# Turning every block of B.x on ScalarE and DMA: a fused S5 and long-convolution kernel

## The chip, the cores and the metric

One NeuronCore of a Trainium2 chip. The metric is the device time of one execution in microseconds (us), the median of several runs.

## The reference, cut to what matters

With x of 2048 rows and 1024 columns, the result is `g*a + (1-g)*b`:

```
g = sigmoid((x * gate_w).sum(-1))
a = S5(x):   Bu = x @ B_bar^T (complex, 1024 states);  h[t] = Lam_bar*h[t-1] + Bu[t]
             a = 2*Re(h @ C^T) + x*Dskip
b = H3(x):   kv = shift(k)*v;  b = x * (long_conv(kv, ssm_k) + kv*ssm_D)      # FFT of length 4096
```

The recurrence is taken two steps at a time. For a pair of rows the kernel forms `V = even + Lam*odd_before` (complex), scans over the pairs, and rebuilds the other half of the states from the scanned ones. `V` is what this text calls a *turned* block: the even half of `B.x` plus the odd half, one step back, times a complex number per state.

## The kernel before, in words

**Tiles.** x is cut into 4 time blocks (tb) of 512 rows, each split into an even and an odd half of 256 (HB). The states are cut into 4 groups (g) of two tiles (j) of 128. So `B.x` has 16 blocks (tb, g), numbered by `order`: blocks 0 to 5 are (0,0), (0,1), (1,0), (1,1), (2,0), (2,1), then (0,2), (0,3), (1,2), (1,3), (2,2), (2,3), and the last four are time block 3. A block's tile, one j, costs 32 matmuls of 256 columns (as separate halves, names `odd` and `even`) or 16 of 512 columns (name `both`).

**Engines.** TensorE (PE) multiplies; ScalarE (ACT) moves nearly every PSUM result to SBUF; VectorE (DVE) does the products of the spectra and the scans; GpSimd (POOL) issues the DMAs that add to what lies in their destination (`gather`, line 133); SyncE (SP) issues the loads, the transposing loads and the stores. PSUM is one pool of 4 buffers of two banks each (`ps2`), so a PE tile can only start when the buffer four tiles earlier has been copied out.

**Order.** Every instruction is recorded through `put`, which pins it behind the one recorded before it on its engine. So each engine runs in the order in which the program text calls it, written out by hand with generators (`step`, `steps`, `run`): if an instruction waits, all later ones of its engine wait too. All recorded instructions show the one line L94, and are told apart by the names of their tiles.

**First half: the long convolution.** Channel blocks c = 0 to 7 go through `fwd_K` (matmuls `psk`, copied out as `Kh` or `BT`), `fwd_V` (`psv`, copied out as `Vh`), `products(c)` on DVE (the `G`, `wkh`, `t` and `BT` rows), and `inverse(c-1)` (`psz`, copied out as `cv` and stored to the DRAM scratch `cv_scr`). Each turn of the loop has one `mirror` matmul, which waits for DVE's `ks`. Between these lie tiles of `B.x` for blocks 0 to 3 (the generator `parts`) and 4 and 5 (the generator `tiles`).

**How a block is turned.** There are two ways.

- Blocks 0 and 1 (`Bu_tile`): PE itself adds the turned odd half into the PSUM buffer of the even half, by 4 matmuls a tile with diagonal matrices `lamd`. `lam_diag` builds those, 6 of 128x128 for each group: for group 0 on ACT (`on_act`), for group 1 on DVE.
- Blocks 2 to 15: `Bu_halves` or `Bu_plain` copies both halves out plainly as `O_` and `V_`. A later `turn_U` scales the odd half on ACT into two buffers `Q` (2 instructions of 128x512 for the first, 4 of 128x256 for the second), and each Q is added to `V_` by one gather. The second gather of a block waits until the first has landed, since both add to the same bytes. Rows show these as `Q<-U,lam` and `U<-Q`.

**From the last channel block on.** After the loop, block 6 is made by the tiles b6 and b7, block 7 by b8 and b9, block 8 by b10 and b11; blocks 9 to 13 follow as B9 to B13 of `plan`, while the scans begin. Block 8 uses a buffer of the pool `wu` (3 buffers, shared with Q): its first instruction, `U<-ends`, can only run when an earlier buffer's gathers have landed. Then `psy` matmuls multiply the states by C.

**C's tiles.** `turn_C(pi)` turns tile pi of C (128 states) by `mc2i`, `c2r` and `mc2r`: ACT writes two scaled copies m or Q (128x1024 each), then the tile itself is scaled twice, by ACT for pi 0 and 1 and by DVE (`ts`) for the rest; for pi 0, 1, 4, 5 (`by_sum`) the copies are added by two gathers, for the others by DVE. `on_act` is a list of steps of `turn_C` that `Bu_next` takes between tiles of `B.x`.

**Loads.** `load_BT(g, c)` transposes one part (real or imaginary) of a group of B, 256 states, into `BT[g]`.

Of the kernel before, what the change touches and what calls it, by code (L numbers as in the profile page):

```python
# [20 lines left out]
def kernel(  # L21
# [35 lines left out]
    ND = D // 128  # L57
# [187 lines left out]
    def load_BT(g, c, held=False):  # L245
        if held:
            hold(BT[g][:, c, 0, 0:1])
        load_t(BT[g][:, c], (A_B_re, A_B_im)[c][g * 256:(g + 1) * 256, :])

    def load_xT(tb, halves=(0, 1), held=False):  # L250
        if tb not in xTs:
# [515 lines left out]
    order += [(NTB - 1, g) for g in range(NG)]  # L767
    ends = consts.tile([128, 2, NG, 2, 2], BF16, name="ends")

    def lam_diag(g, home, on_act=False):  # L770

        if g == 0:
            lamd["all"] = home.tile([128, 2, 2, 3, 128], BF16, name="lamd", tag="lamd")
        t = lamd[g] = lamd["all"][:, g]
        for j in range(2):
            for k, f in enumerate((lam[:, 0], lam[:, 1], mlam)):
                pi = 2 * g + j
                if on_act:
                    act(t[:, j, k], ident, func=ACT.Identity, scale=f[:, pi:pi + 1])
                else:  # L780
                    ts(t[:, j, k], ident, f[:, pi:pi + 1], None, ALU.mult)

    def Bu(i):
        tb, g = order[i]
        if i == 13:
            V_ = s5p["v13"].tile([128, 2, 2, HB], BF16, name="V13")
            O_ = lam_pool.tile([128, 2, 2, HB + 2], BF16, name="O13", tag="lamd")
            Us[tb, g] = V_, O_[:, :, :, 2:]
            turns_U[i] = turn_U(g, V_, O_)
            return [Bu_plain(tb, g, V_, O_, j) for j in range(2)]  # L790
        if i in (10, 11):
            if i == 10:
                s5p["u2"] = xt_pool.tile([128, 2, 2 * (4 * HB + 4)], BF16, name="U2", tag="xT")
            U = s5p["u2"][:, i - 10]
        else:
            shape = [128, 2 * (4 * HB + 4)]
            if i in (6, 7, 8, 15):
                U = u4(shape, BF16, "U")
            else:
                home = uu[0 if i in (0, 1, 14) else 1] if i < 6 or i == 14 else s5p["uu"]  # L800
                U = home.tile(shape, BF16, name="U")
        if i >= 2:
            V_, O_ = U[:, 0:4 * HB], U[:, 4 * HB:]
            V_ = V_.rearrange("p (c j t) -> p c j t", c=2, j=2)
            O_ = O_.rearrange("p (c j t) -> p c j t", c=2, j=2)
            Us[tb, g] = V_, O_[:, :, :, 2:]
            turns_U[i] = turn_U(g, V_, O_)
            return [(Bu_halves if i < 4 else Bu_plain)(tb, g, V_, O_, j) for j in range(2)]
        U = U[:, 0:8 * HB].rearrange("p (a c j t) -> p a c j t", a=2, c=2, j=2)
        Us[tb, g] = U[:, 0], U[:, 1]  # L810
        return [Bu_tile(tb, g, U, j) for j in range(2)]

    def Bu_tile(tb, g, U, j):
        xT = xTs[tb]
        ps = []
        d = lamd[g][:, j]
        for a in (1, 0):
            ps.append(ps2([128, 2, HB], ("even", "odd")[a]))
            for c in range(2):
                for dt_ in range(ND):  # L820
                    mm(ps[1 - a][:, c], BT[g][:, c, dt_, j * 128:(j + 1) * 128], xT[:, dt_, a * HB:(a + 1) * HB],
                       dt_ == 0 and (a == 1 or c == 0), a == 1 and dt_ == ND - 1)
            if a == 1:
                act(U[:, 1, :, j], ps[0], func=ACT.Copy)
                if j == 1 and tb < NTB - 1:
                    act(ends[:, tb % 2, g], U[:, 1, :, :, HB - 1], func=ACT.Copy)
                yield
        yield
        for k, c, o in ((0, 0, 0), (0, 1, 1), (1, 0, 1), (2, 1, 0)):
            if tb > 0:  # L830
                mm(ps[1][:, o, 0:1], d[:, k], ends[:, 1 - tb % 2, g, c, j:j + 1], False, False)
            mm(ps[1][:, o, 1:HB], d[:, k], U[:, 1, c, j, 0:HB - 1], False, k == 2)
        act(U[:, 0, :, j], ps[1], func=ACT.Copy)
        yield

    turns_U = {}

    def Bu_halves(tb, g, V_, O_, j):
        if j == 0:
            act(O_[:, :, :, 1], ends[:, 1 - tb % 2, g], func=ACT.Copy)  # L840
        for a in (1, 0):
            ps = ps2([128, 2, HB], ("even", "odd")[a])
            for c in range(2):
                for dt_ in range(ND):
                    mm(ps[:, c], BT[g][:, c, dt_, j * 128:(j + 1) * 128], xTs[tb][:, dt_, a * HB:(a + 1) * HB],
                       dt_ == 0, dt_ == ND - 1)
            if a == 1:
                act(O_[:, :, j, 2:], ps, func=ACT.Copy)
                if j == 1:
                    act(ends[:, tb % 2, g], O_[:, :, :, HB + 1], func=ACT.Copy)  # L850
            else:
                act(V_[:, :, j], ps, func=ACT.Copy)
            yield
        yield

    def Bu_plain(tb, g, V_, O_, j):
        xT = xTs[tb]
        if j == 0 and tb > 0:
            act(O_[:, :, :, 1], ends[:, 1 - tb % 2, g], func=ACT.Copy)
        elif j == 0:  # L860
            act(O_[:, :, :, 1], lam[:, :, 0:2], func=ACT.Copy, scale=0.0)
        ps = ps2([128, 2, 2, HB], "both")
        for c in range(2):
            for dt_ in range(ND):
                mm(flat(ps[:, c]), BT[g][:, c, dt_, j * 128:(j + 1) * 128], xT[:, dt_], dt_ == 0, dt_ == ND - 1)
        act(O_[:, :, j, 2:], ps[:, :, 1], func=ACT.Copy)
        if j == 1 and tb < NTB - 1:
            act(ends[:, tb % 2, g], O_[:, :, :, HB + 1], func=ACT.Copy)
        act(V_[:, :, j], ps[:, :, 0], func=ACT.Copy)
        yield  # L870

    def turn_U(g, V_, O_):
        both = slice(0, 2)
        for part in (((both, both, lam[:, 0]),), ((0, 1, lam[:, 1]), (1, 0, mlam))):
            if s5p["Q"] is s5p["wu"]:
                if part[0][0] == both:
                    whole_Q = u4([128, 2, 2, 2, HB], BF16, "Q")
                Q = whole_Q[:, part[0][0] != both]
            else:
                Q = s5p["Q"].tile([128, 2, 2, HB], BF16, name="Q")  # L880
            for j in range(2):
                pi = 2 * g + j
                for c, o, f in part:
                    act(Q[:, o, j], O_[:, c, j, 1:1 + HB], func=ACT.Identity, scale=f[:, pi:pi + 1])
            gather(V_, Q)
            yield
# [211 lines left out]
    step(sp)  # L1098
    run(first)
    dg1 = dgs(1, True)  # L1100
    run(angles)
    load("kT", 1)
    load("v", 1)
    load("kn", 1)
    fwd_K(0, (0, 1))
    fwd_V(0, (0, 1))
    step(sp)
    step(turns)
    taps(1, dg1)
    step(sp)  # L1110
# [21 lines left out]
    for c in range(NC - 1):  # L1132
        n, nn = c + 1, c + 2
        if c == 0:
# [28 lines left out]
            step(apart)  # L1163
            load_xT(0, (1,))
            run(apart)
            lam_diag(0, lam_pool, True)
            continue
        if c == 6:
            put("pool", nc.gpsimd.tensor_copy, stamp, xTs[2][:, 0, 0:HB + 1:HB])
# [1 line left out]
        step(old)  # L1171
        step(tabs)
        if c == 6:
            step(parts)
        step(back)
        step(tv)
        steps(prod, 3)
# [11 lines left out]
        if c == 2:  # L1189
            step(parts)  # L1190
        fwd_K(n, (0, 1))
        if c in (2, 6):
            step(parts)
        fwd_K(n, (2, 3))
        if c == 4:
            step(parts)
# [6 lines left out]
        if nn < NC:  # L1203
# [2 lines left out]
            step(fk)  # L1206
            if c < 5:
                step(fk)
            if c == 4:
                step(parts)  # L1210
            if c == 1:
                load_BT(1, 0, True)
            elif c < 5:
                load("v", nn, True)
            step(parts)
            taps(nn, dg)
            if c == 5:
                load("v", nn)
# [20 lines left out]
        else:  # L1239
            run(next(tiles))  # L1240
            for pi in range(3):
# [2 lines left out]
                    hold(CT[0][:, 0, 0:1])  # L1244
                load_CT(pi)
                if pi == 0:
                    load_BT(2, 0)
                    load_BT(2, 1)
            run(next(tiles))
            run(next(tiles))  # L1250
        fwd_V(n, (0, 1))
        if c < 6 and c != 4:
            step(parts)
            if c in (1, 3):
                step(parts)
        fwd_V(n, (2, 3))
        if c in (4, 5):
            step(parts)
        if c == 1:
            lam_diag(1, lam_pool)  # L1260
        old = tabs

    h3r.close()
# [10 lines left out]
    def turn_C(pi):  # L1274
# [7 lines left out]
            act(m[c], CT[pi][:, 1 - c], func=ACT.Identity, scale=mc2i[:, pi:pi + 1])  # L1282
            yield
        for c, f in enumerate((c2r, mc2r)):
            if pi < 2:
                act(CT[pi][:, c], CT[pi][:, c], func=ACT.Identity, scale=f[:, pi:pi + 1])
            else:
                ts(CT[pi][:, c], CT[pi][:, c], f[:, pi:pi + 1], None, ALU.mult)
            if by_sum:
                gather(CT[pi][:, c], m[c])  # L1290
        if not by_sum:
            tt(CT[pi], CT[pi], whole_m, ALU.add)

    turning = [turn_C(pi) for pi in range(NP)]
    load_BT(3, 0)
    load_BT(3, 1)
    load_CT(3)
    with tc.tile_pool(name="fin", bufs=1, side="right") as fin:

# [5 lines left out]
        prod, back = products(c, 0, room, False), inverse(c - 1)  # L1305
        run(old)
        steps(prod, 3)
        run(turns_U[3])
        run(next(tiles))
        steps(turning[0], 2)  # L1310
        step(back)
        steps(turning[1], 2)
        run(back)
        gate(1)
        gate(2)
        steps(prod, 2)
        b6, b7 = Bu(6)
        run(b6)
        run(b7)
        run(turns_U[6])  # L1320
        run(turning[0])
# [111 lines left out]
    for j in range(NS):  # L1433
# [6 lines left out]
        advance(j)  # L1440
        for t in turning[2 * j:2 * j + 2]:
            run(t)
        on_act += [lambda t=t: step(t) for t in turning[2 * j + 2:2 * j + 4] for _ in range(2)]
        turn = turns_U[turned[j]] if j in turned else none
        if j != 10 and plan[j][0:1] != "G":
            step(turn)
# [82 lines left out]
```

## Time and profile before

| | |
|---|---|
| median of 3 runs | 384.49 us (384.44 to 384.77) |
| the profiled execution | 384.57 us: its span 382.8 us, and 1.8 us around it |
| granted TensorE clock | 0.998 |
| busy PE / DVE / ACT / POOL | 371.3 / 371.2 / 303.6 / 81.8 us |
| DMA | 71.77 MB, 187 GB/s on average |

How to read it: busy time is the sum of the instructions' durations on an engine, and the span is the time from the first instruction to the last. Instructions of one engine overlap at their ends (an ACT row of 0.60 us is followed by the next one 0.49 us after its start), so costs in the text are taken from start to start where a row of the same kind follows. The chain is found by going back from the last instruction to what released it. "Idle before" is time in which an engine did nothing ahead of an instruction, with what ended it.

### The profile page before, as it was taken

Reading aid. Unit: us, or ns where it says so; the run is one execution under the profiler, and the core shown is the slowest. Engines: PE = TensorE matmul, PEld = TensorE weight load, DVE = VectorE, ACT = ScalarE, POOL = GpSimd, SP = SyncE. Lnnn points to the kernel's source line nnn. Section 1 sums busy time; section 2 is a strip of 40 time slices with the busy share of each in tenths; the row PEclk is TensorE's granted clock in tenths of the full one; section 3 lists DMA queues with packets and bytes.
Section 4 is the critical chain, followed back from the end, with each engine's and each line's share of the span. In section 5 each row is a group of like instructions: output and inputs, shape, how many; then the busy total and the mean of one; then the engine's idle time right before and its main releaser. Section 6 shows DMA issues by size and latency. Waiting matters only on the chain.

```text
span 382.8 us, 6633 instructions
## 1 busy us (share of the span) xinstructions
PE 371.3 (97%) x2419; PEld 198.3 (52%) x2453; DVE 371.2 (97%) x599; ACT 303.6 (79%) x469; POOL 81.8 (21%) x108
## 2 busy tenths in 40 slices
PE   7899999999999999999999999989999999999995
PEld 5566458575584846744454444434444444444442
DVE  7999999999999999999999999999999999999996
ACT  5898998988979999786979699675989759937601
POOL 4011030020301102031003110413414323634100
PEclk9999999999999999999999999999999999999999
DMA  7979999998999997959999999986899999898903
GB/s 166 165 108 223 218 205 205 245 203 211 201 164 211 208 213 169 198 125 154 192 221 164 226 203 250 213 153 125 150 222 192 208 245 246 136 250 156 238 8 110
DMA packets 126402, 71.77 MB, mean 187 GB/s; under 512 B 104665, under 2 KB 107489, under 8 KB 126370
## 3 DMA queue, kind: packets, MB, share of 16 engines
q1 hardware_dynamic: 111232, 45.64, 55.4%
q0 software_dynamic: 12976, 25.17, 38.9%
q10 hardware_dynamic: 2162, 0.54, 0.8%
q8 instruction: 19, 0.31, 0.3%
q14 instruction: 13, 0.11, 0.1%
HBM read 15.48 MB, written 8.39 MB: 62 GB/s over the span
## 4 chain that ended last, share of the span: by engine, by line
PE 52%; DVE 30%; issue 9%; DMA 4%; ACT 3%; ACTq 1%; POOL 0%; DVEq 0%; POOLq 0%
PE psy L94 29%; PE both L94 15%; DVE BT L94 11%; DVE wkh L94 8%; DVE G L94 5%; DVE t L94 3%; PE psz L94 2%; DVE ks L94 2%; PE psk L94 2%; DMA CT<-Q 2%; DMA pbb<-cv_scr 1%; PE psv L94 1%; DMA rows<-in_gate_w_dram 1%; PE p L94 1%; PE taps L94 1%
## 5 line engine op out<-in xcount | busy, mean ns | idle before, releaser
L94 PEld LDWEIGHTS <-BT 128*128 128x128 bf16 x640 | 62.0, 98 | 48.3 <-issue 0.2
L94 PE MATMUL both<-xT,BT 128*128 128x512 bf16 x375 | 83.0, 379 | 0.4
L94 POOL DMA_DIRECT2D U<-Q x26 | 26.7, 1039 | 88.8 <-ACT Q L94 31.0
L94 PEld LDWEIGHTS <-hb 128*128 128x128 bf16 x256 | 24.9, 98 | 31.4 <-issue 1.6
L94 PEld LDWEIGHTS <-U 128*128 128x128 bf16 x240 | 23.5, 98 | 28.3
L94 PE MATMUL psy<-CT,hb 128*128 128x512 bf16 x157 | 36.3, 379 | 0.1
L94 ACT ACTIVATE Vh<-psv 128x1024 bf16<-128x1024 f32 x32 | 30.7, 1034 | 5.3 <-PE psv L94 5.3
L94 PE MATMUL psy<-CT,U 128*128 128x512 bf16 x149 | 34.6, 379 | 0.2
L94 ACT ACTIVATE Q<-U,lam 128x512 bf16<-128x512 bf16 (+1 forms) x52 | 29.9, 612 | 4.9 <-DMA CT<-Q 4.9
L94 DVE TENSOR_TENSOR_SCAN W<-rv,init,A 128x256 bf16<-128x256 f32 x48 | 32.2, 730 | 0.0
L94 POOL DMA_DIRECT2D G<-wkh x8 | 9.7, 1218 | 102.8 <-DVE wkh L94 102.8
L94 ACT ACTIVATE U<-both 128x512 bf16<-128x512 f32 x44 | 24.1, 595 | 8.0 <-PE both L94 7.5
L94 PEld LDWEIGHTS <-SF 128*128 128x128 bf16 x184 | 18.0, 98 | 19.7 <-issue 1.4
L94 PE MATMUL psk<-eok,SF 128*128 128x512 bf16 (+1 forms) x119 | 27.9, 354 | 0.3
L94 PE MATMUL psz<-G,CI 128*128 128x512 bf16 x64 | 24.3, 379 | 0.1
L94 PE MATMUL psz<-G,SI 128*128 128x512 bf16 x64 | 24.3, 379 | 0.0
L94 PE MATMUL psy<-CTa,hb 128*128 128x512 bf16 x94 | 22.6, 379 | 1.2 <-ACT U L94 1.0
L94 PE MATMUL taps<-dg,kT 128*128 128x128 bf16 (+1 forms) x352 | 21.7, 210 | 0.8 <-DMA kT<-in_B_k_dram 0.8
L94 PEld LDWEIGHTS <-kT 128*128 128x128 bf16 x352 | 21.0, 100 | 2.5 <-DMA kT<-in_B_k_dram 2.1
L94 DVE TENSOR_TENSOR wkh<-BT,Vh 128x3072 bf16<-128x3072 bf16 (+4 forms) x20 | 21.8, 1110 | 0.0
L94 DVE TENSOR_TENSOR wkh<-Kh,Vh 128x3072 bf16<-128x3072 bf16 (+2 forms) x16 | 21.2, 1348 | 0.0
L94 PE MATMUL psy<-CTa,U 128*128 128x512 bf16 x87 | 20.4, 379 | 0.1
(227 smaller groups left out, 846.1 us busy)
## 6 DMA issues: line engine op xcount, KB each, us to landing
U<-Q POOLq DMA_DIRECT2D x26, 256.0 KB, 5.3
G<-wkh POOLq DMA_DIRECT2D x6, 768.0 KB, 8.8
cv_scr<-cv SPq DMA_DIRECT2D x16, 256.0 KB, 5.7
kn<-in_B_ssm_k_dram SPq DMA_DIRECT2D x5, 512.0 KB, 4.0
v<-in_B_v_dram SPq DMA_DIRECT2D x5, 512.0 KB, 6.2
out_dram<-m SPq DMA_DIRECT2D x8, 256.0 KB, 4.5
BT<-cv_scr SPq DMA_DIRECT2D x7, 256.0 KB, 5.9
out_dram<-BT SPq DMA_DIRECT2D x7, 256.0 KB, 2.0
```

Source lines behind the costliest of these rows:

```text
L94: i = f(*a, **kw)
```

## The change

It has four parts.

1. **Blocks 0 and 1 are made as blocks 2 and 3 are.** `lam_diag` and `Bu_tile` go, with their 12 small instructions and 16 matmuls. `Bu_halves` now takes a list of halves, and one half may be cut in two PSUM tiles (block 1, odd, j = 1). Blocks 0 and 1 get a `turn_U` each. `turns_U[0]` runs at the start of c = 6, with the table NCF, no longer needed, and a small new tile `Qb` as its Q buffers; `turns_U[1]` takes the place of `turns_U[3]` in the last channel block; `turns_U[3]` moves between the tiles b6 and b7, with NCF and Qb again; `turns_U[6]` follows b7 as before.
2. **PE's order of `B.x`.** Tiles are spread otherwise over the loop (256-column matmuls before the mirrors of c = 2 to 6: 48, 56, 56, 48, 48, where it was 48+4, 48+8, 48+4, 48, 64 with the matmuls by `lamd` as the second number), and in the last part the fourth tile of blocks 4 and 5 stands ahead of `psv`, and gates 1 and 2 ahead of `psz`.
3. **B's groups 2 and 3** are loaded by four transposes of 128 states each instead of two of 256.
4. **C's tiles 4 and 5** are scaled by ACT instead of DVE, four instructions of 128x1024; their first step comes one tile of `B.x` sooner. In the first microseconds, half of `fwd_K(0)` and the angles are reordered around `state_params` (`sp`, the rates).

The diff, cut to its core:

```diff
+    def load_BT_halves(g):
+        for j in range(2):
+            for c in range(2):
+                rows = slice(g * 256 + j * 128, g * 256 + (j + 1) * 128)
+                load_t(BT[g][:, c, :, j * 128:(j + 1) * 128], (A_B_re, A_B_im)[c][rows, :])
...
-    def lam_diag(g, home, on_act=False):
...
-    def Bu_tile(tb, g, U, j):
...
+        turns_U[i] = turn_U(g, V_, O_)
+        if i < 4:
+            halves = (((1, 0), (1, 1), (0, 0), (0, 1)) if i == 2 else ((1, 0), (0, 0), (1, 1), (0, 1)))
+            return [Bu_halves(tb, g, V_, O_, [(a, j, (i, a, j) == (1, 1, 1)) for a, j in halves])]
+        return [Bu_plain(tb, g, V_, O_, j) for j in range(2)]
...
+            elif s5p["Q"] is None and part[0][0] == both:
+                Q = NCF.rearrange("p o (j t) -> p o j t", j=2)
+            elif s5p["Q"] is None:
+                Q = lam_pool.tile([128, 2, 2, HB], BF16, name="Qb", tag="lamd")
...
-    run(angles)
...
-    fwd_K(0, (0, 1))
+    fwd_K(0, (0,))
+    step(sp)
+    run(angles)
+    fwd_K(0, (1,))
     fwd_V(0, (0, 1))
-    step(sp)
...
         if c == 6:
-            step(parts)
+            s5p["Q"] = None
+            run(turns_U[0])
         step(back)
...
-                    load_BT(2, 0)
-                    load_BT(2, 1)
+                    load_BT_halves(2)
+            run(next(tiles))
             run(next(tiles))
             run(next(tiles))
         fwd_V(n, (0, 1))
...
-            if pi < 2:
+            if by_sum:
                 act(CT[pi][:, c], CT[pi][:, c], func=ACT.Identity, scale=f[:, pi:pi + 1])
             else:
                 ts(CT[pi][:, c], CT[pi][:, c], f[:, pi:pi + 1], None, ALU.mult)
             if by_sum:
                 gather(CT[pi][:, c], m[c])
+                yield
...
-        run(turns_U[3])
-        run(next(tiles))
+        run(turns_U[1])
+        gate(1)
+        gate(2)
         steps(turning[0], 2)
         step(back)
         steps(turning[1], 2)
         run(back)
-        gate(1)
-        gate(2)
         steps(prod, 2)
         b6, b7 = Bu(6)
         run(b6)
+        s5p["Q"] = None
+        run(turns_U[3])
+        s5p["Q"] = s5p["wu"]
         run(b7)
         run(turns_U[6])
...
-        on_act += [lambda t=t: step(t) for t in turning[2 * j + 2:2 * j + 4] for _ in range(2)]
+        if j > 0:
+            on_act += [lambda t=t: step(t) for t in turning[2 * j + 2:2 * j + 4] for _ in range(4 if j == 1 else 2)]
```

More of the change, by code (lines that the diff above doesn't have):

```diff
@@ L768 @@
     ends = consts.tile([128, 2, NG, 2, 2], BF16, name="ends")
-    def lam_diag(g, home, on_act=False):
[L772 to L781, printed above, removed]
     def Bu(i):
@@ L801, in Bu @@
                 U = home.tile(shape, BF16, name="U")
[L802 to L809, printed above, removed]
@@ L810, in Bu @@
-        Us[tb, g] = U[:, 0], U[:, 1]
-        return [Bu_tile(tb, g, U, j) for j in range(2)]
-    def Bu_tile(tb, g, U, j):
[L814 to L826, printed above, removed]
-                yield
[L828 to L834, printed above, removed]
@@ L836 @@
-    turns_U = {}
-    def Bu_halves(tb, g, V_, O_, j):
-        if j == 0:
-            act(O_[:, :, :, 1], ends[:, 1 - tb % 2, g], func=ACT.Copy)
[L841 to L854, printed above, removed]
+        V_, O_ = U[:, 0:4 * HB], U[:, 4 * HB:]
@@ new lines, in Bu @@
+        V_ = V_.rearrange("p (c j t) -> p c j t", c=2, j=2)
+        O_ = O_.rearrange("p (c j t) -> p c j t", c=2, j=2)
+        Us[tb, g] = V_, O_[:, :, :, 2:]
+        turns_U[i] = turn_U(g, V_, O_)
[3 more added lines that the diff above has]
+        return [Bu_plain(tb, g, V_, O_, j) for j in range(2)]
+    turns_U = {}
@@ new lines, in Bu_halves @@
+    def Bu_halves(tb, g, V_, O_, parts):
+        before(tb, g, O_)
+        for a, j, split in parts:
+            for cs_ in ((0,), (1,)) if split else ((0, 1),):
+                ps = ps2([128, 2, HB], ("even", "odd")[a])
+                for c in cs_:
+                    for dt_ in range(ND):
+                        mm(ps[:, c], BT[g][:, c, dt_, j * 128:(j + 1) * 128], xTs[tb][:, dt_, a * HB:(a + 1) * HB],
+                           dt_ == 0, dt_ == ND - 1)
+                cc = slice(cs_[0], cs_[-1] + 1)
+                act(O_[:, cc, j, 2:] if a == 1 else V_[:, cc, j], ps[:, cc], func=ACT.Copy)
+                if a == 1 and j == 1 and cs_[-1] == 1:
+                    act(ends[:, tb % 2, g], O_[:, :, :, HB + 1], func=ACT.Copy)
+                yield
@@ L856, in Bu_plain, with before @@
+    def before(tb, g, O_):
+        if tb > 0:
+            act(O_[:, :, :, 1], ends[:, 1 - tb % 2, g], func=ACT.Copy)
+        else:
+            act(O_[:, :, :, 1], lam[:, :, 0:2], func=ACT.Copy, scale=0.0)
     def Bu_plain(tb, g, V_, O_, j):
         xT = xTs[tb]
[L858 to L861, printed above, removed]
+        if j == 0:
+            before(tb, g, O_)
@@ L1165 @@
             run(apart)
-            lam_diag(0, lam_pool, True)
             continue
@@ L1191 @@
         fwd_K(n, (0, 1))
-        if c in (2, 6):
-            step(parts)
         fwd_K(n, (2, 3))
@@ L1208 @@
                 step(fk)
-            if c == 4:
-                step(parts)
             if c == 1:
@@ L1214 @@
                 load("v", nn, True)
-            step(parts)
+            steps(parts, 2 if c == 3 else 1)
             taps(nn, dg)
@@ L1251 @@
         fwd_V(n, (0, 1))
-        if c < 6 and c != 4:
+        if c < 4:
             step(parts)
-            if c in (1, 3):
-                step(parts)
         fwd_V(n, (2, 3))
-        if c in (4, 5):
+        if c == 5:
             step(parts)
-        if c == 1:
-            lam_diag(1, lam_pool)
         old = tabs
@@ L1294 @@
     turning = [turn_C(pi) for pi in range(NP)]
-    load_BT(3, 0)
-    load_BT(3, 1)
+    load_BT_halves(3)
     load_CT(3)
```

## The prediction

> **What bounds the kernel now.** I read the page first (busy times, chain by engine), then the chain in order of time, then the timelines of each engine around its turns. About 0.2% (0.77 us) is what a measurement here can tell from no change.
>
> The page, busy times and the chain by engine:
>
> ```profile
> PE 371.3 (97%) x2419; PEld 198.3 (52%) x2453; DVE 371.2 (97%) x599; ACT 303.6 (79%) x469; POOL 81.8 (21%) x108
> PE 52%; DVE 30%; issue 9%; DMA 4%; ACT 3%; ACTq 1%; POOL 0%; DVEq 0%; POOLq 0%
> ```
>
> PE and DVE are both full, so the average does not say which of them sets the end. The chain (start, us, what) does, by stage:
>
> ```profile
> 144.62 2.20 DVE BT L94
> 158.44 2.28 DVE BT L94 x2
> 164.74 1.89 PE psz L94 x8
> ...
> 244.74 5.78 DMA CT<-Q
> 253.15 9.01 PE psy L94 x41
> 262.21 10.74 PE psy L94 x49
> ```
>
> From 32 to 164 us it runs over DVE's products, from the mirror at 164.3 us to the end over PE, broken once by a chain of DMAs and ACT before 253.15. PE's timeline shows each side waiting for the other:
>
> ```profile
> 94.79 0.60 PE L94 MATMUL mirror<-ks,refl 128*128 128x512 bf16 x2 [0.37 <-DVE ks L94]
> 253.15 1.02 PE L94 MATMUL psy<-CTa,hb 128*128 128x512 bf16 x4 [1.04 <-ACT U L94]
> ```
>
> The mirrors wait 0.15 to 0.4 us for DVE; in the PE-bound stretch the one gap is 1.04 us at 253.15, where `psy` waits for ACT to copy out block 12. So what the second half is worth is read from ACT between 185 and 254 us:
>
> ```profile
> 213.41 0.22 ACT L94 ACTIVATE U<-ends 128x4 bf16<-128x4 bf16 x1 [2.26 <-DMA U<-Q]
> 250.54 1.34 ACT L94 ACTIVATE Q<-U,lam 128x512 bf16<-128x512 bf16 x2 [4.92 <-DMA CT<-Q]
> ```
>
> and from POOL's gathers, which feed the first of those waits:
>
> ```profile
> 203.24 0.86 POOL L94 DMA_DIRECT2D U<-Q  x1 [9.84 <-ACT Q L94]
> 207.93 0.86 POOL L94 DMA_DIRECT2D U<-Q  x1 [3.83 <-ACT CTa L94]
> 208.60 3.72 POOL L94 DMA_DIRECT2D CTa<-m  x4
> ```
>
> Block 6's first gather goes out at 203.24, its second when the first has landed, and that one lands at 213.41, when ACT may write block 8.
>
> **The change, first half.** Removed from PE: 16 matmuls by `lamd`, 0.44 us for each four, 1.75 us in all. They lie where DVE is the bound, and PE waits for DVE at the mirrors, so this alone is worth nothing. ACT's six `lamd` (0.295 us each, 1.8 us) stand beside DVE's work likewise: nothing. DVE's six, from 70.66 to 71.64 (0.98 us), are on the chain. But the next products need the last `Vh`. At 117.66 `G` starts 0.30 us after it. In that turn PE gets 56 instead of 48 matmuls of 256 columns (8 x 0.109 = +0.87) and loses four by `lamd` (-0.44): +0.43; its mirror before can come 0.37 earlier at most (the wait at 94.79). So `G` can start at 117.66 - 0.30 - 0.37 + 0.43 = 117.42: of 0.98, 0.25 us is kept. Bounds 0 and 0.98. The mirror of c = 6 then comes at 164.05. `turn_U(0)` on ACT (2 x 0.62 + 4 x 0.40 = 2.82 us, as from 185.93 to 188.75) falls between 160.6 and 164, where ACT idles 0.63 + 0.85 + 1.13 and has one tile less to copy: nothing; without that cover `cv` and the mirror's copy would be up to 2.8 us late, which `ev` on DVE (at 170.2) would not see. The reorder at the start removes DVE's 1.0 us wait for `rv`, but ACT is without a gap from 22 to 32 us and DVE then waits for its `Vh`: nothing.
>
> **Second half: ACT's queue.** PE's matmuls from the mirror on are the same in number, so the end moves by the mirror and by stalls. Step by step, from before's starts:
>
> - `psv` now stands behind the fourth tile: it ends at 184.54 + 3.45 - 0.25 = 187.74 instead of 184.5. ACT copies the last `Vh` from 188.25 to 189.3. DVE wanted it at 189.17 - 0.25, so DVE loses its 0.25 again; it is not the bound here.
> - ACT: `turn_U(1)` 189.15 to 191.97; gates 0.2; four m of 1.04 and two `cv` of 0.91 to 1.0, 198.2; 0.2 for block 6's border; b6's copies 0.98, so 199.4. There `turn_U(3)` begins, new in this place. From a turn's start to its first gather's issue the rows give 1.62 to 1.66 (201.62 to 203.24): the NCF gather goes out at 201.05.
> - POOL, in order: the Qb gather waits for NCF's landing. Issue to next issue of such a pair took 4.69, 4.95, 5.23 and 6.01 (203.24, 187.59, 172.86, 220.15): 206.0. Behind it, 0.7 later (207.93 to 208.60), block 6's first gather at 206.7, though ACT has its Q ready by 205.1. Its second follows 5.2 later at 211.9, and lands 5.48 later as before, with C's four gathers behind it: 217.4. Bounds: 4.69 three times and 0.67 from 201.05 give 215.8; 6.01, 0.86, 6.7 (the median of the overlapped `CT<-Q`) and 6.0 give 220.6.
> - ACT comes to `U<-ends` at 212.85 (turns, four CTa of 1.04, five copies) and so waits 4.5 us instead of 2.26. Everything behind it on ACT waits too: block 8's copies, two `cv`, the turn of block 7, C's m, and PE, whose tile `both` of block 9 needs block 8's PSUM buffer, 1.4 us after the landing: 218.8, where PE would be there at 217.0.
> - From that landing ACT has 213.41 to 253.15 = 39.74 us, less its idle 4.92 + 0.70 + 0.14, = 33.98 us of work up to the copy that releases `psy`. C's tiles 4 and 5 add 4 x 1.04 = 4.16: 38.1. The 4.92 us wait for `CT<-Q` vanishes, since these gathers now go out over 10 us ahead of their buffer's reuse. `psy` starts at 217.4 + 38.1 = 255.5 instead of 253.15.
>
> On DVE the four `ts` from 243.96 to 245.55 go (1.59 us). PE is the bound from there on, and `CT6` and `CT7` need ACT's m at about 248 and 251, just when DVE would come to them: nothing. That the first step on C's tiles comes sooner is inside the 38.1. After 253.15 PE has no gap to give back, so the sum is 384.57 + 2.35 = 386.9 us by the profiled execution, 0.08 above the median shown.
>
> The half transposes: two of 256 states held SP 3.66 and 2.31 us (`BT`, from 179.90), a tile of C of the same bytes as a half 1.3. Four halves cost 4 x 1.3 = 5.2 or, at the other end, 4 x 3.66 = 14.6, against 6.0. I take the first: a half has the bytes of C's row. The other end would bring B's group 3 some 10 us late to b8 at 200 us, as nothing covers it there.
>
> Only the gathers' price comes from another place also. The Trainium skill, "DMA: Bandwidth & Descriptors", section on the anatomy of one DMA on the SWDGE path, fits a DMA by 2.0 us plus its bytes over 436 GB/s. An estimate from that page for 256 KB is 2.6 us, where this trace has 5.3 (median to landing); by 2.6 the last gather would land at about 210, ahead of ACT, and the end would be that of the first rival.
>
> **Rivals.** The decision lies in one point: `psy` starts 38.1 us after block 6's second gather lands, so the change is slower if that is after 253.15 - 38.1 = 215.05.
>
> *Faster: the gathers land before ACT asks.* If they land by 213.75, PE runs through and loses also its 1.04 us: `psy` at 253.15 - 1.04 - 0.25 = 251.86, the end at 384.57 - 1.29 = 383.3; with all 0.98 kept 382.6. For it: ACT could be earlier at `turn_U(3)`, for its order was reconstructed over 15 us, and a 2.3 us slip upstream suffices. Against: four rows of pairs, none under 4.69.
>
> *DVE is the bound all along.* Then 0.98 + 1.59 = 2.57 us come off: 382.0. For it: DVE's 97%, and the Trainium skill's "Perfetto Trace Analysis", "Optimizing Scalar/DVE Operations", by which moving work from a saturated DVE to ScalarE may pay. Against: the chain has no DVE in it from 164 us on, and ACT's instruction costs 1.04 where DVE's costs 0.40.
>
> *No difference.* Landing between 214.3 and 215.8, a little under my lower bound: about 384.6.
>
> *Slower still.* Overlapped gathers at the upper bounds, or late half transposes: 220.6 + 38.1 = 258.7, the end at 390.1.
>
> **How the numbers follow.** Landing at 215.8 to 219.5 (end 385.3 to 389.0) 0.55, later 0.07: slower 0.62. No difference 0.12. Faster 0.26, of which 0.04 for DVE as the bound. The predicted time is that of the likeliest, 386.9. The range reaches down to 383.0, into the first rival, and up to 389.0; it leaves out the upper end and the lower part of the faster cases, under 2 in 10. The likeliest case's own range is 385.3 to 389.0.
>
> **What would show it.** Right: ACT's `U<-ends` at about 217 with a wait of 4 to 5 us for `U<-Q`; a PE gap of 1.5 to 2 us ahead of `both` there; two `U<-Q` issues under 1 us apart near 206; no wait for `CT<-Q`; `psy` at 255 to 256 behind ACT; the mirror of c = 6 at 164.0. Wrong: `psy` at or before 253 with no wait, a `U<-ends` that waits under 1 us, or PE gaps elsewhere, for B's half loads above all.

## The result and the profile after

| | before | after |
|---|---|---|
| median | 384.63 us (384.44 to 387.51, 6 runs) | 388.97 us (388.32 to 393.74, 6 runs) |
| ratio, with its 95% interval | | 1.0145 (1.0108 to 1.0182) |
| the profiled execution | 384.57 us, span 382.8 | 388.78 us, span 387.0 |
| granted TensorE clock in it | 0.998 | 0.993 |

The granted clock is the share of TensorE's full speed that the profile shows it to have had. The change makes the kernel slower. The same kernel was run twice more on other occasions, beside the kernel before: 389.13 us median, ratio 1.0106 (1.0071 to 1.0141), called the control below, and 389.06 us, ratio 1.0085 (1.0053 to 1.0116), called the third. Ratios leave disturbed executions out, so they can differ from the ratio of two medians.

The page after, busy times and the chain by engine:

```profile
PE 373.6 (97%) x2437; PEld 197.6 (51%) x2437; DVE 369.7 (96%) x589; ACT 313.1 (81%) x482; POOL 85.3 (22%) x112
PE 42%; issue 2%; DMA 1%; ACT 0%; DVE 0%; DVEq 0%; ACTq 0%; POOLq 0%
```

DVE lost 1.5 us of work and ACT gained 9.5, yet neither says anything about the 4.2 us between the two profiled executions. The chain does (start, us, what):

```profile
207.37 1.20 DMA U<-Q
208.57 7.26 issue
215.85 3.30 DMA U<-Q
...
219.23 0.23 ACT U L94
...
220.62 36.38 PE both L94 x160
...
257.01 27.79 PE psy L94 x128
```

Block 6's two gathers now lie on the chain that ends last; behind them come ACT's first write of block 8, PE's tile of block 9, and `psy` at 257.01 instead of 253.15. POOL's timeline and SP's show how those gathers came to be there. Rows are start, duration, engine, operation and tiles, and in brackets the idle time before and its releaser:

```profile
201.90 0.86 POOL L94 DMA_DIRECT2D U<-NCF  x1 [4.63 <-ACT NCF L94]
206.83 0.86 POOL L94 DMA_DIRECT2D U<-Qb  x1 [4.08 <-issue]
207.37 1.20 POOL L94 DMA_DIRECT2D U<-Q  x1
215.85 0.86 POOL L94 DMA_DIRECT2D U<-Q  x1 [7.28 <-issue]
```

SP's loads of x for time block 3, first in the profile before, then after:

```profile
207.25 6.78 SPq L94 DMA_TRANSPOSE xT<-in_A_x_dram  x2
```

```profile
207.79 7.37 SPq L94 DMA_TRANSPOSE xT<-in_A_x_dram  x2
```

The gather of NCF holds Qb's back until 206.83, and block 6's first gather queues behind Qb's, 4.1 us later than before (207.37 against 203.24; how much of this is the queue and how much ACT's order is measured below). There it meets the two transposing loads of `xT`, which the earlier first gather had preceded by 4 us. Its pair takes 8.48 us where it took 4.69. ACT's and PE's rows show the price:

```profile
219.23 0.22 ACT L94 ACTIVATE U<-ends 128x4 bf16<-128x4 bf16 x1 [5.40 <-DMA U<-Q]
```

```profile
220.62 1.35 PE L94 MATMUL both<-xT,BT 128*128 128x512 bf16 x4 [2.90 <-ACT U L94]
164.64 0.61 PE L94 MATMUL mirror<-ks,refl 128*128 128x512 bf16 x2 [0.37 <-DVE ks L94]
```

The second PE row is the mirror of c = 6, at 164.30 before: in this execution the first half gained nothing, PE having lost 1.07 us to a load (`kT`) at 60.75.

### The profile page after: what moved, and what is told of

It reads as the page before. It is cut to its first block, busy times and chain, and to the rows that moved or that the text cites. A ratio compares the mean times of both kernels' runs of the same rounds, so it can differ in the third digit from the quotient of the medians.

```text
span 387.0 us, 6650 instructions
## 1 busy us (share of the span) xinstructions
PE 373.6 (97%) x2437; PEld 197.6 (51%) x2437; DVE 369.7 (96%) x589; ACT 313.1 (81%) x482; POOL 85.3 (22%) x112
## 5 line engine op out<-in xcount | busy, mean ns | idle before, releaser
L94 PE MATMUL both<-xT,BT 128*128 128x512 bf16 x384 | 85.2, 384 | 2.9 <-ACT U L94 2.9
L94 POOL DMA_DIRECT2D U<-Q x26 | 28.1, 1080 | 77.0 <-ACT Q L94 21.2
```

What stands on the lines that cost most here:

```text
L94: i = f(*a, **kw)
```

## The experiments

"Pair" is the time from the issue of block 6's first gather to that of its second, "both" the time from the first issue to ACT's `U<-ends`. The time in parentheses is that of the profiled execution.

**The control.** The changed kernel, unaltered.

> The changed kernel once more, as the control on the same chip as the three beside it. Every theory: 388 to 394 us, and in its trace ACT's U<-ends at 219 to 221 us behind U<-Q.

```profile
206.75 1.20 POOL L94 DMA_DIRECT2D U<-Q  x1
213.53 0.86 POOL L94 DMA_DIRECT2D U<-Q  x1 [5.58 <-ACT U L94]
```

389.13 us (387.88). Pair 6.78, `U<-ends` at 218.41, `psy` at 256.16. The first half is 0.42 us ahead here (mirror 163.88), so the mirror moves by more from run to run than the change moves it.

**Block 3 turned without its two gathers.** The turn's instructions on ACT stay; its two gathers are left out, so block 3's states stay unturned.

```diff
-            gather(V_, Q)
+            if add:          # add is False for block 3
+                gather(V_, Q)
```

> The changed kernel with the two gathers of block 3's turn left out (ACT still writes NCF and Qb, but block 3 stays unturned, so the output is not the reference's). ACT's work is unchanged. Theory (block 6's gathers queue behind those two and share the DMA engines with the second): its first gather issues when ACT has the Q, at about 206, the second about 5 us later, it lands at about 216 instead of 219, psy starts at about 254, and the time is 385.5 to 386.5 us, 2.5 us or more under the control. Rival (ACT's load alone): no change from the control.

```profile
205.39 0.86 POOL L94 DMA_DIRECT2D U<-Q  x1 [8.45 <-ACT Q L94]
211.60 0.86 POOL L94 DMA_DIRECT2D U<-Q  x1 [5.35 <-ACT U L94]
```

386.51 us (386.46), ratio 1.0019 (0.9979 to 1.0059). The first gather goes out 1.36 us before the control's, as POOL is free; `U<-ends` comes at 217.02, 1.39 earlier, and `psy` at 254.77, 1.39 earlier. So the queue behind NCF and Qb is worth 1.4 us by the profiles and 2.6 by the medians. What stays is instructive: 205.39 is still 2.15 later than in the kernel before, which is ACT's new order, and "both" is 11.63 us as in the control (11.66), though no gather of Qb is near.

**The loads of xT moved behind the last store to `cv_scr`.** This asks whether those loads or Qb's gather slow the pair. The same move was made in the changed kernel, in the kernel before, and in a partial version (below).

```diff
-        load_xT(3)              # between b9 and b10
...
     back = inverse(c)
     step(back)
     run(back)
+    load_xT(3)
```

> The changed kernel, with the two transposing loads of xT for time block 3 issued after the last channel block's second store to cv_scr (about 222 us) instead of at 207. Theory: the pair of block 6's gathers is slow because its first gather now goes out less than 1 us ahead of these two loads (4 us ahead of them in the kernel before, where the pair took 4.69). Then the pair takes 5.4 to 5.8 us (with Qb's gather still beside it), the second goes out at about 212.3 and lands at 217, psy starts at 254.8, and the end comes 1.3 us before that of the changed kernel, 2.5 with the faster landing. Rival: Qb's gather beside it is what slows it; the pair stays at 6.7 to 8.5 us and the time within 0.5 us of the changed kernel's. Price if the loads become late themselves: C's and the scans' loads behind them on SP move from 224 to about 231, which would show as a wait of ACT's m or of DVE after 240.

> The changed kernel once more, as it is, to stand beside the kernel with xT late on the same chip. Both theories: a ratio of 1.010 to 1.015 to the kernel before, pair of block 6's gathers 6.7 to 8.5 us, landing 218.4 to 219.2.

> The kernel before with the same loads moved behind the store. Theory: block 6's first gather had no such load beside it (pair 4.69, stays at 4.4 to 5.0), but the second had, and lands in 4.5 instead of 5.5 us: U<-ends at about 212.4 instead of 213.4. psy there waited 1.04 us behind the four CT gathers and not behind this landing alone, so at most 1 us comes off: 383.5 to 384.6. Rival: no load matters to a gather, 384.6; or the loads behind it on SP are late, 385 to 387.

The changed kernel with the move, POOL and then ACT; and ACT of the kernel before with it:

```profile
209.82 0.86 POOL L94 DMA_DIRECT2D U<-Qb  x1 [7.52 <-ACT CTa L94]
210.36 1.20 POOL L94 DMA_DIRECT2D U<-Q  x1
215.10 0.86 POOL L94 DMA_DIRECT2D U<-Q  x1 [3.54 <-issue]
```

```profile
218.47 0.22 ACT L94 ACTIVATE U<-ends 128x4 bf16<-128x4 bf16 x1 [5.10 <-DMA U<-Q]
238.82 2.19 ACT L94 ACTIVATE Q<-CT,mc2i 128x1024 bf16<-128x1024 bf16 x2 [7.79 <-DMA CT<-in_A_C_im_dram]
```

```profile
211.63 0.22 ACT L94 ACTIVATE U<-ends 128x4 bf16<-128x4 bf16 x1 [0.37 <-DMA U<-Q]
```

With Qb's gather 0.54 us ahead of it as in the control, the pair takes 4.74 us, and without any gather of Qb but with `xT` beside it, it took 6.21 (above): the loads of `xT` slow it, and Qb's gather does not. In the kernel before the pair hardly changes (4.96) and the second gather, which had those loads beside it, lands at 211.63 instead of 213.41. But the end gets no better: 385.14 us, ratio 1.0003 (0.9974 to 1.0032), for the kernel before, where ACT now waits 2.61 and 1.77 us for loads of C, and 395.62 us, ratio 1.0262 (1.0213 to 1.0311), for the changed one, since the loads of C behind `xT` on SP now come 7 us later and ACT waits 7.79 us for them. In the changed kernel with the move the pair of NCF and Qb took 8.38 us instead of 5.09, with the same loads in flight as in the control. This is not explained; so `U<-ends` came no earlier than in the control (218.47 against 218.41), and the run shows the price of the pair but no gain at the end. It also shows that a pair can be that slow with no load of `xT` near. The third run of the changed kernel, on the same chip, had pair 6.64 and "both" 11.62.

**Block 3 turned elsewhere.** If the queue is the matter, another place for `turns_U[3]` should help. Three were tried: behind b9; at the early place, right after a first tile of blocks 4 and 5; and later than block 7's turn, a step of `plan` behind it (there with `psv` ahead of the fourth tile and C's tiles by DVE again).

```diff
         run(b6)
-        s5p["Q"] = None
-        run(turns_U[3])
-        s5p["Q"] = s5p["wu"]
         run(b7)
...
         run(b9)
+        s5p["Q"] = None       # behind b9; the early place: after the first run(next(tiles));
+        run(turns_U[3])       # the last: turned[1] = 3
+        s5p["Q"] = s5p["wu"]
```

> The changed kernel with one edit: the turn of block 3 (turns_U[3], gathers from NCF and Qb) runs after the tile b9 instead of between b6 and b7, so block 6's gathers have POOL's queue and the DMA engines to themselves. Theory (the gather queue: block 6's second gather landing late at 219.2 us costs the time): its first gather issues at about 203.6, the second lands at about 214, ACT's U<-ends waits under 1 us, the 3 us gap of PE ahead of block 9's tile is gone, psy starts at about 252.5, and the time is 384.2 us (383.6 to 385). Rival (ACT has 7 us more to do before psy, in whatever order): the same work is there, so 388 to 389 us as in the changed kernel.

> The changed kernel with one edit: block 3's turn (NCF and Qb) right after the first tile of blocks 4 and 5 in the last turn of the loop, at about 177 us, where ACT idles 0.9, 2.0 and 2.4 us between the copies of the tiles and POOL has nothing to issue. Theory (block 6's gathers must not queue behind others): block 6's first gather issues at about 203.6, the second at 208.6, it lands at about 214, psy could start at 214 + 37.8 = 251.8 by ACT, PE comes there at 252.5, and the time is 383.5 to 384.5 us: level with before or a little under it. Rival (the DMA engines are short in this stretch, so four more gathers of 256 KB delay the loads of C and B wherever they stand): ACT's m waits for CTa, PE for BT, and the time is 386 to 389 us.

> The changed kernel with three edits: PE's order of the last channel block as before (psv ahead of the fourth tile, gates behind psz); block 3's turn around the tiles B9 and B10 of the plan, behind block 7's turn; C's tiles 4 and 5 scaled by DVE, but at the sooner place. Theory (the landing of block 6's gathers plus ACT's work behind it): ACT and POOL do the same as before up to block 8, so block 6 lands at about 214; ACT's work behind it is 34.0 + 2.8 = 36.8 us, so psy could start at 250.8, and PE comes there itself at 252.4: 383.5 to 384.8 us, level with before or a little faster. Rival (four gathers and two turns more cost wherever they stand): 386 us or more.

All three are slower than the kernel before: 398.44 us (391.22), ratio 1.0233 (1.0131 to 1.0334); 391.67 us (391.70), ratio 1.0082 (1.0038 to 1.0125); 397.91 us (393.63), ratio 1.0224 (1.0180 to 1.0268). The first and the last ratio rest on two executions of the variant each. My theory, that the gathers cost only what is queued behind them, missed each time. The early place, POOL, ACT and PE:

```profile
182.86 1.20 POOL L94 DMA_DIRECT2D U<-NCF  x1
192.03 0.86 POOL L94 DMA_DIRECT2D U<-Qb  x1 [7.97 <-DMA U<-NCF]
```

```profile
199.17 2.19 ACT L94 ACTIVATE m<-CTa,mc2i 128x1024 bf16<-128x1024 bf16 x2 [3.83 <-DMA CTa<-in_A_C_im_dram]
```

```profile
204.19 2.32 PE L94 MATMUL both<-xT,BT 128*128 128x512 bf16 x5 [4.56 <-DMA BT<-in_A_B_re_dram]
```

Here the gathers of block 3 meet the loads of C and of B's group 3; the pair takes 9.17 us and the loads are late for ACT and PE. Block 6's own pair took 6.71 us there, though the loads of `xT` came 7.75 us behind its first gather; loads of B and C went out within 2.5 us of that gather on either side. Behind b9 the loads were late too (ACT 3.24 us for `CTa` at 198.50, PE 1.83 and 0.89 for `BT`), though no gather of block 3 had gone out by then: in that run block 1's own pair, from 190.73, took 8.04 us (4.72 in the control) and the last load of `CTa` beside it 4.0 us (1.4). So loads and gathers collide there by chance too, and the experiment does not show what the place itself costs. Later on the gathers of NCF and Qb met block 7's. In the last place ACT waited 5.77 us for `CT` at 251.89, since the memory of NCF serves a later pool and SP stood until 236.64 for its gather.

**The order on PE and ACT.** `psv` again ahead of the fourth tile, and the gates behind `psz`, as in the kernel before.

```diff
             run(next(tiles))
-            run(next(tiles))
         fwd_V(n, (0, 1))
...
         run(turns_U[1])
-        gate(1)
-        gate(2)
+        run(next(tiles))
```

> The changed kernel with PE's order of the last channel block put back: psv ahead of the fourth tile of blocks 4 and 5, gates 1 and 2 behind psz. The turn of block 1 then starts about 3.3 us earlier on ACT, at 186.6, and DVE does not wait for its last Vh at 190. Theory (gather queue): the NCF gather issues about 2 us sooner than 201.9 as ACT still takes the fourth tile's copies behind the turn, block 6 lands at about 217, and the time is 386.5 us (385.8 to 387.5). Rival (the overlap of two gathers, 8.5 us for the first, is what counts and not where the queue starts): the same 2 us. Rival (ACT's load): no change, 388.5 us.

389.78 us (387.87), ratio 1.0115 (1.0067 to 1.0162): a miss. ACT did come earlier to `turn_U(1)`, but then waited 1.58 us for `CTa` at 194.32; Qb's gather went out at 205.65 against 206.21, and "both" took 12.22 us.

**Turn 3 split about turn 6.** NCF's gather early, Qb's behind block 6's pair.

```diff
-        run(turns_U[3])
+        step(turns_U[3])
...
         run(turns_U[6])
+        run(turns_U[3])        # with Qb
```

> The changed kernel with the second half of block 3's turn (Qb, four instructions of 0.40 us and a gather) behind block 6's turn, the first half (NCF) left in its place. Theory (queue and overlap): block 6's first gather issues when ACT has its Q, at about 204.5, beside NCF's, which is almost landed by then; its second issues at about 210, with Qb's and C's four behind it, and lands at 215.5 to 217; psy at 253.3 to 254.8, 385.2 to 386.7 us. Rival (only the sum of the gathers' bytes ahead of the landing counts): Qb's gather shares the engines with the second one, it lands at about 219 as in the changed kernel, and the time is 388 us or more.

388.98 us, ratio 1.0061 (1.0022 to 1.0101): at best a part of the loss comes back. The profiled execution took 398.46 us and does not stand for that median, so nothing is read from it.

**The other parts.** C's tiles 4 and 5 by DVE again in the changed kernel; the same part alone, by ACT, in the kernel before; and the half loads of B with the reordered start alone, in the kernel before.

```diff
-            if by_sum:        # changed kernel; the other way round in the kernel before
+            if pi < 2:
                 act(CT[pi][:, c], CT[pi][:, c], func=ACT.Identity, scale=f[:, pi:pi + 1])
...
-    load_BT(3, 0)             # the kernel before, half loads (group 2 likewise)
-    load_BT(3, 1)
+    load_BT_halves(3)
```

> The changed kernel with C's tiles 4 and 5 scaled by DVE again (four instructions of 0.40 us there, 4.16 us less on ACT). Theory (gather queue): block 6 still lands at about 219 and PE still idles about 3 us there; from 220.6 PE has 160 matmuls, 34.5 us at full rate, so psy cannot start before 255.1, and the time is 386.5 to 388.8 us, depending on how long PE runs at half rate after its gap. Rival (ACT's load, by the sum of the prediction): psy at 219.2 + 34.0 = 253.2 and 384.7 us.

> The kernel before with one part of the change: C's tiles 4 and 5 scaled by ACT, first step a tile sooner. Theory: the 4.16 us on ACT lie in its 4.92 us wait for CT<-Q, which goes, so psy starts within 0.8 us of before and the time is 384.0 to 385.3 us. Rival (DVE is the bound): 1.6 us faster, 382.9 us. Rival (ACT's load costs in full): 2 to 4 us slower, 386.5 us or more.

> The kernel before with B's groups 2 and 3 loaded by four half transposes each, and the reorder of the first microseconds (rates sooner). Theory: SP is held 6.2 us by four halves where two wholes held it 5.4 to 6.0, and the first microseconds end on ACT either way: the same time within 0.2%. Rival (late loads cost): PE waits for BT<-in_A_B at block 6 and the time is 1 to 2 us above before.

389.12 us (390.03), ratio 1.0081 (1.0048 to 1.0114): no different from the control, so the rival by ACT's load (384.7) is out. In the kernel before, 386.87 us, ratio 1.0026 (0.9994 to 1.0059), above the 384.0 to 385.3 expected, and 385.28 us, ratio 1.0022 (0.9987 to 1.0057): neither part can be told from no change. By the first of these, DVE as the bound is refuted, as C's scaling on ACT would then have gained 1.6 us. The profile of C by ACT in the kernel before (386.98 us) shows PE waiting 2.43 us at 153.97 for a load (`kT`) that this part does not touch, so such waits come and go without any edit near them.

**Block 1 alone.** The kernel before with block 1 as plain halves, turned at c = 6 from NCF and Qb; block 0 stays with `lamd`, DVE's six small instructions go, and PE's order stays. Then the same with C's tiles by ACT, and that with the loads of `xT` moved (both edits as shown above).

```diff
-        if i >= 2:
+        if i >= 1:
...
         if c == 6:
             step(parts)
+            run(turns_U[1])
...
-        if c == 1:
-            lam_diag(1, lam_pool)
```

> The kernel before with half of the change's first part: block 1 is made plainly and turned at the start of c = 6 from NCF and Qb, block 0 stays with the matmuls by lamd; DVE's six lamd instructions go; nothing else moves, block 3's turn stays where it was. Theory: the two added gathers lie at 163 to 172 us, away from block 6's; DVE's 0.98 us is kept in part (0.25 to 0.5), block 6 lands at 213 to 214 as before, psy starts at 252.7 to 253.2: 383.9 to 384.6 us, no difference that can be told. Rival (every gather of 256 KB in the second half of the convolution delays C's and B's loads): ACT's m waits for CTa or PE for BT, 385.5 us or more.

> The same with C's tiles 4 and 5 scaled by ACT. Theory (38.1 us of ACT's work behind block 6's landing, without the wait for CT<-Q): psy at 213.5 + 37.8 = 251.3 by ACT, 251.9 by PE, so its 1.04 us stall goes: 383.0 to 384.0 us, 0.2 to 0.4% under before. Rival (the loads are late): 385.5 us or more. Rival (DVE bound): 382.4 us.

> The kernel before with block 1 alone turned by ScalarE, C's tiles 4 and 5 by ScalarE, and the same loads of xT moved behind the store. Theory: the landing comes at about 213.5 instead of 214.5 and psy needs no wait in either, so within 0.3 us of that kernel (profiled 384.0) unless PE's wait for cv (1.4 us) shrinks too; ratio to the kernel before 0.995 to 1.000. Rival: loads behind it late, ratio over 1.002.

```profile
163.40 0.39 PE L94 MATMUL mirror<-ks,refl 128*128 128x512 bf16 x1 [0.21 <-DVE ks L94]
```

```profile
194.80 2.19 ACT L94 ACTIVATE m<-CTa,mc2i 128x1024 bf16<-128x1024 bf16 x2 [2.62 <-DMA CTa<-in_A_C_im_dram]
```

385.66 us (385.27), ratio 0.9970 (0.9933 to 1.0007): the mirror comes 0.90 us sooner (and at 163.14 and 163.08 in the other two), nearly all of DVE's 0.98, but two gathers more make the load of `CTa` 2.62 us late (it was not waited for before). With C by ACT it is 385.70 us (384.02), ratio 0.9992 (0.9946 to 1.0037), `psy` at 252.58 without a wait; with `xT` late besides, 393.13 us, ratio 1.0164 (1.0108 to 1.0221), ACT waiting 5.72 us for `CT`. The first is the best version found, and cannot be told from the kernel before.

## Why the prediction was right and wrong

The direction and the mechanism were right: block 6's second gather sets ACT, then block 9's tile, then `psy`. The size was short: 386.9 us against 388.78, 387.88 and 388.17 in the three profiled executions, that is +2.3 us against +4.2, +3.3 and +3.6. The predicted ratio, 386.9 / 384.57 = 1.0061, lies in the interval of the third run only.

- **The mis-sized term is block 6's pair of gathers**, put at 5.2 us from four rows of pairs. It took 8.48, 6.78 and 6.64. They were rows of the same kind in other company, and what SP would have in flight at 206.7 had no place in the sum; the row at 207.25 in the profile before answers that. Even the upper bound for a pair, 6.0, was passed. The landing was then quicker than the 5.48 assumed (3.38, 4.88 and 4.98), probably as the loads were over or nearly so, and gave part of it back: that the landing, at 218.4 to 219.2, stayed within the likeliest case's 215.8 to 219.5 was in part luck. For both gathers together I had 10.7 us; the runs give:

| kernel | first gather | loads of xT start | Qb's gather ahead | pair | both |
|---|---|---|---|---|---|
| before | 203.24 | 207.25 | no | 4.69 | 10.17 |
| after | 207.37 | 207.79 | yes | 8.48 | 11.86 |
| control | 206.75 | 207.69 | yes | 6.78 | 11.66 |
| block 3 without gathers | 205.39 | 206.81 | no | 6.21 | 11.63 |
| after, xT late | 210.36 | 223.29 | yes | 4.74 | 8.11 |
| before, xT late | 203.36 | 220.29 | no | 4.96 | 8.27 |

  The other variants bear this out. Where `xT`'s loads start within 2 us behind the first gather, the pair takes 6.2 to 8.5 us in six profiles of six (with C by DVE 6.73, with PE's order put back 6.90). Where they start 4 us or more behind it, it takes 4.4 to 5.8 us in ten profiles; the eleventh is the early place, with 6.71 us and loads of B and C beside it. Each is one execution, and the profile of the split turn is left out as above.

- **NCF's issue, Qb's and block 6's first** were put at 201.05, 206.0 and 206.7: 201.90, 206.83 and 207.37 after, 201.12, 206.21 and 206.75 in the control. The steps hold (4.93 and 5.09 between NCF and Qb, for 4.95); the start of the chain in the result is late by 0.85, of which 0.59 came with the first half (mirror 164.64 for 164.05).
- **From the landing to `psy`, 38.1 us**: 37.78 from `U<-ends` after, 37.75 in the control and without the gathers of block 3. Right, and so was the vanished wait for `CT<-Q`.
- **The sum** then closes. After: 0.67 us for the later first gather, 1.16 for both gathers (11.86 for 10.7), -0.32 from there to `psy`, and 0.34 for the end (387.0 - 257.01 = 129.99, before 382.8 - 253.15 = 129.65): 386.9 + 1.85 = 388.75, measured 388.78.
- **The loss, by cause**, from before to the control: `U<-ends` comes 5.00 us later, 2.15 from ACT's order, 1.36 from the queue behind NCF and Qb, and the rest, 1.49, from slower gathers ("both" 11.66 for 10.17), which is put down to the collision with `xT`. Of these 5.00, `psy` keeps 3.01, since ACT's later waits vanish. Medians of other runs are up to 1.3 us above the profiled executions, and two runs of the result, at 393.4 and 393.7 us, had no profile: this part stays open.
- **The first half.** 0.25 us was to be kept, mirror at 164.05: it came at 164.64, 163.88 and 164.16, and between 163.74 and 164.51 in the other variants with that first half whose profiles are read here, so about that, within what runs differ. The reason given holds: DVE does wait for the last `Vh` in the changed kernel,

```profile
117.99 2.29 DVE L94 TENSOR_TENSOR G<-BT,Vh 128x4096 bf16<-128x4096 bf16 x1 [0.54 <-ACT Vh L94]
```

  and with PE's order left alone (block 1 alone) 0.90 is kept. In the last channel block DVE waited 0.37 us for `Vh` at 190.15, where the prediction's times make 0.38 (189.3 less 188.92), and as put this cost nothing.
- **PE's gap** ahead of block 9 was put at 1.5 to 2 us: 2.90, 1.78 and 2.21.
- **The half transposes** were put at 5.2 us; group 3's four took 1.25 + 1.82 + 1.70 + 1.31 = 6.1. The control and the third run show PE waiting 0.9 and 0.5 us for one, ahead of ACT's longer wait, so it cost nothing. The rates and C's sooner step were nothing, as put.
- **The rivals.** The gathers did not land by 213.75 in any profile of the changed kernel, nor as late as 220.6. DVE as the bound is refuted above. An estimate by the Trainium skill's fit, "DMA: Bandwidth & Descriptors", section on the anatomy of one DMA on the SWDGE path, is 2.6 us for such a gather. No gather of this kind landed in under 3.2 us in any trace here, and block 6's pair took at least 4.4 from issue to issue, so no run here reaches it.
- **What I had no term for at all**: the DMA engines themselves. In each variant that put block 3's gathers, block 1's or `xT`'s loads elsewhere, the longest wait of PE or ACT for a load was 2.2 to 7.8 us, and four gathers more are what this change adds. That the engines are short is argued from this, not shown: such waits come by chance too (2.43 us for `kT` above). In the profile before, DMA share is 1.10 from 195 to 225 us, against 1.14 after (it adds up the queues, so it can pass 1): the engines were as full before. The Trainium skill's "DMA: Bandwidth & Descriptors", section "Issuing engines are not separate DMA queues", says that DMAs of all engines interleave on the same 16 engines; these runs agree, with block 6's pair, issued by POOL, at 4.7 to 5.0 us in the table where SP's loads of `xT` stay clear of it and at 6.2 to 8.5 where they don't.

## What to carry to other kernels

When a DMA moves, price it by a row of the same kind that had the same company, and list what every other queue has in flight at the new place: here the row that mattered stood in SP's timeline, not in POOL's. Work taken from a saturated engine is free only if the transfers that come with it are: 0.98 us saved on DVE brought four gathers, and in each place tried for them another load came late, by chance or not. To find which neighbour is to blame, move the neighbour: leaving the gathers out showed the queue, and only moving `xT` showed the collision, though it made other loads late and saved nothing.

## What was not expected of the hardware

PE runs at half its rate for some 3.4 us after some of its gaps of 2.1 us or more, and not after others. The stretches after a gap: in the changed kernel, in the one with C by DVE, and in the early place, behind its gap of 4.56 us (the last three columns are the granted clock, the DMA share and GB/s):

```profile
core 0: us, PE busy (x) PEld busy (x) DVE busy (x) ACT busy (x) POOL busy (x), PEclk, DMA share, GB/s
216.00:220.00 4.00, 1.72 (x8) 0.69 (x7) 3.97 (x9) 0.74 (x3) 4.00 (x5) 1.00 0.91 166
220.00:225.00 5.00, 4.38 (x13) 1.66 (x13) 4.90 (x13) 4.97 (x10) 0.24 (x1) 0.66 1.09 211
```

```profile
222.00:227.00 5.00, 4.86 (x14) 1.89 (x15) 4.93 (x10) 4.97 (x11) 0.40 (x1) 0.66 0.99 231
```

```profile
204.00:209.00 5.00, 4.81 (x12) 1.79 (x13) 4.93 (x7) 4.99 (x10) 0.86 (x1) 0.50 0.91 165
```

The last row, behind the longest of these gaps, is half rate throughout its 5 us, 0.50, and so is the changed kernel from 221.6 to 223.6 us. So a clock of 0.66 over 5 us is half rate for 3.4 of them. The shortest gap that it followed is one of 2.10 us, in the variant with block 3 turned last:

```profile
198.72 19.11 PE L94 MATMUL both<-xT,BT 128*128 128x512 bf16 x80 [2.10 <-ACT cv L94]
```

Over the 5 us behind that gap the clock is 0.66, and so it is, or nearly (up to 0.68), behind gaps of 2.43, 2.50, 2.58, 2.73, 2.82, 2.90 and 3.43 us in other profiles. It stayed at 1.00 behind gaps of 1.78, 2.21, 2.46, another of 2.82, 2.96 and 2.99, so the length alone does not decide. Blocks 9 to 13's 160 matmuls took 36.38 us after, and 34.69 where the gap was 1.27. It cost nothing further in the changed kernel, where ACT released `psy` at the same moment, but with C by DVE PE alone was late. The Trainium skill, "TensorE: Matmul & The Clock Gate", section "What's actually happening", puts the idle time after which the clock is halved, and the busy time until it is full again, each at a window of about 3.4 us, free-running. Here 2.10 us of idle was enough once and 2.99 was not, while the 3.4 us until full rate agree.
